# The order of all five engines taken from a list scheduler, in a kernel of decayed attention and a gated layer

## The chip, the cores and the metric

The kernel runs on one core of a Trainium2 chip. Times are microseconds of device time of one execution; the time of a kernel is the median over its runs. The core's engines are TensorE (PE, with its weight loads PEld), VectorE (DVE), ScalarE (ACT), GpSimd (POOL) and SyncE (SP), which here only issues transfers. Each runs its own instructions in the order in which the program wrote them, and waits where an operand is not there yet.

## The reference

Inputs q, k and v have 4 batches, 8 heads, 768 positions and 64 features in float32. With a decay per head, `lam`, and blocks of positions:

```python
intra = einsum(qb, kb) * Dmask;  intra = einsum(intra, vb)
inter = einsum(qb * lam_pow, kv_state)
out[block] = intra + inter
kv_state = lam_block * kv_state + einsum(kb * rev_pow, vb)
```

The attention output, with its 8 x 64 features side by side, is x with 3072 rows of 512, and the gated layer makes the result of it:

```python
H = maximum(x @ w_h, 0);  T = sigmoid(x @ w_t + b_t)
return T * H + (1 - T) * x
```

## The kernel before, in words

Work goes by chunks of 128 positions: 6 in a batch, 24 in all. The heads are taken in 4 pairs, so that a pair's features fill 128 partitions. Decay is factored: values are scaled by a negative power of lam (`pow_k`), the products are taken without decay, and the sum is scaled by a positive power (`pow_q`), so that the mask is a plain triangle (`tri`).

For chunk n the stages are, with the lines of the kernel before:

- SP loads keys (L55), values (L60), and for each pair of chunks the queries (L65). The 8 pieces of the two weight matrices come between chunk 1 and chunk 2 (L85). Up to `LA` = 10 chunks lie ready.
- POOL casts keys (`cast_k`, L140) and queries (`cast_q`, L153) to bf16 and scales values (`scale_v`, L145).
- PE transposes keys (L166) and queries (L159) into one PSUM buffer `tr`; ACT copies them out (`kT` L168, `qT` L161).
- PE makes scores (L179), DVE masks them (L182). PE multiplies the state by the queries (`inter`, L189) and adds the masked scores times the values (`intra`, L196); DVE scales that by `pow_q` into `xT` (L202).
- PE adds the chunk to the state (L211), ACT copies it for the next chunk (`s_bd`, L215).

Two chunks form a group for the gated layer; the last two chunks are groups of one. For a group, in two halves of the output features, PE multiplies by w_h (L223, an h half), DVE takes maximum and difference (`hmx`, L226), PE multiplies by w_t (L235, a t half), ACT takes the sigmoid (L239), DVE multiplies (`thmx`, L242). Then for each chunk PE turns the sum of `xT` and `thmx` back to rows (`ffn_out`, L250, a turn), ACT copies it out (`o_sb`, L254; DVE L256 for two of the last), and SP stores it (L257). Each PSUM tile has one buffer, so an h half waits for the `hmx` of the one before it.

The order on each engine is that of the calls at the end of the function (L279 to L342): a written start for chunks 0 to 4, then a loop whose step i casts chunk i + 3, transposes the keys of i + 2, makes the scores of i + 1, does the rest of i, transposes the next query pair in even steps, does one half of the gated layer (`ffn_step`, L261) with one turn between its h and its t, and loads chunk i + 10. The gated layer takes a group from a list, `units`, that `close` fills (L273). ACT makes the table `pow_q` in eight operations (L126).

Of the kernel before, what the change touches and what calls it, by code (L numbers as in the profile page):

```python
# [12 lines left out]
ALU = mybir.AluOpType  # L13


@with_exitstack
def kernel(
# [20 lines left out]
    LA = 10  # L38
    sizes = [2] * (N // 2 - 1) + [1, 1]
    first = [sum(sizes[:g]) for g in range(len(sizes))]  # L40
    group = [g for g, z in enumerate(sizes) for _ in range(z)]

    ctx.enter_context(tc.manual_schedule())
    singles = ctx.enter_context(tc.tile_pool(name="singles", bufs=1))
    load = ctx.enter_context(tc.tile_pool(name="load", bufs=2))
    work = ctx.enter_context(tc.tile_pool(name="work", bufs=2))
    ps = ctx.enter_context(tc.tile_pool(name="ps", bufs=1, space=bass.MemoryType.PSUM))


    kf, vf, qf = {}, {}, {}  # L50

    def load_k(n):
        b, c = divmod(n, NCH)
        kf[n] = load.tile([C, H, D], F32, tag="kf", name="kf", bufs=LA)
        nc.sync.dma_start(out=kf[n], in_=k[b, :, c * C:(c + 1) * C, :].rearrange("h p d -> p h d"))  # L55

    def load_v(n):
        b, c = divmod(n, NCH)
        vf[n] = load.tile([C, H, D], F32, tag="vf", name="vf", bufs=LA)
        nc.sync.dma_start(out=vf[n], in_=v[b, :, c * C:(c + 1) * C, :].rearrange("h p d -> p h d"))  # L60

    def load_q(s):
        b, c = divmod(J * s, NCH)
        qf[s] = load.tile([128, H, J * D], F32, tag="qf", name="qf", bufs=LA // J)
        nc.sync.dma_start(out=qf[s], in_=q[b, :, c * C:(c + J) * C, :].rearrange("h (p j) d -> p h (j d)", j=J))  # L65

    def loads(n):
        if n < N:
            load_k(n)
            if n % J == 0:  # L70
                load_q(n // J)
            load_v(n)
# [5 lines left out]
    loads(0)  # L78
    loads(1)
    w_f, w_b = [], []  # L80
    for w in (moe_w_h, moe_w_t):
        w_f.append(singles.tile([128, KC, DM], F32, name=f"w_f{len(w_f)}"))
        w_b.append(singles.tile([128, KC, DM], BF16, name=f"w_b{len(w_b)}"))
        for kc in range(KC):
            nc.sync.dma_start(out=w_f[-1][:, kc, :], in_=w[kc * 128:(kc + 1) * 128, :])  # L85
    wh, wt = w_b
    for n in range(2, LA):
        loads(n)


# [10 lines left out]

# [21 lines left out]

    def powers(lo, hi):
        for hp in range(NP):
            nc.scalar.activation(pow_q[:, hp, lo:hi], tq_f[:, lo:hi], AF.Exp, scale=ln_hp[:, hp:hp + 1])  # L126

# [5 lines left out]
    nc.vector.tensor_copy(bt_col, bt_ps)  # L133


    kb, qb, qT, kT, vs, masked, xT, thmx, kv_ps, o_ps = ({} for _ in range(10))

    def cast_k(n, eng=None):
        kb[n] = work.tile([C, H, D], BF16, tag="kb", name="kb", bufs=4)
        (eng or nc.gpsimd).tensor_copy(kb[n], kf[n])  # L140

    def scale_v(n):
        c = n % NCH
        vs[n] = work.tile([C, H, D], BF16, tag="vs", name="vs", bufs=4)
        nc.gpsimd.tensor_tensor(vs[n], in0=vf[n], in1=pow_k[:, :, c, :].to_broadcast([C, H, D]), op=ALU.mult)  # L145

    def cast_q(s, engs=None):
        qb[s] = work.tile([128, J, H, D], BF16, tag="qb", name="qb")
        engs = engs or [nc.gpsimd]
        w = H // len(engs)  # L150
        for i, eng in enumerate(engs):
            h = slice(i * w, i * w + w)
            eng.tensor_copy(qb[s].rearrange("p j h d -> p h j d")[:, h], qf[s].rearrange("p h (j d) -> p h j d", j=J)[:, h])  # L153

    def trans_q(s):
        tr = ps.tile([128, NP, J, 128], BF16, tag="tr", name="tr")
        for hp in range(NP):
            for j in range(J):
                nc.tensor.transpose(tr[:, hp, j, :], qb[s][:, j, 2 * hp:2 * hp + 2, :], id128)  # L159
        qT[s] = work.tile([128, NP, J * C], BF16, tag="qT", name="qT")  # L160
        nc.scalar.activation(qT[s].rearrange("p n (q j) -> p n q j", j=J), tr.rearrange("p n j q -> p n q j"), AF.Copy)  # L161

    def trans_k(n):
        tr = ps.tile([128, NP, C], BF16, tag="tr", name="tr")
        for hp in range(NP):
            nc.tensor.transpose(tr[:, hp, :], kb[n][:, 2 * hp:2 * hp + 2, :], id128)  # L166
        kT[n] = work.tile([128, NP, C], BF16, tag="kT", name="kT", bufs=3)
        nc.scalar.activation(kT[n], tr, AF.Copy)  # L168

    def q_of(n, r, hp):  # L170
        o = n % J * C
        return qT[n // J][r, hp, o:o + C]

    def scores(n):
        s_ps = ps.tile([C, 2, NP, C], F32, tag="s", name="s_ps")
        for hp in range(NP):
            for e in range(2):
                r = slice(64 * e, 64 * e + 64)
                nc.tensor.matmul(s_ps[:, e, hp, :], lhsT=kT[n][r, hp, :], rhs=q_of(n, r, hp), start=True, stop=True)  # L179
        masked[n] = work.tile([C, 2, NP, C], BF16, tag="masked", name="masked")  # L180
        for e in range(2):
            nc.vector.tensor_tensor(masked[n][:, e], in0=s_ps[:, e],  # L182
                                    in1=tri.to_broadcast([C, NP, C]), op=ALU.mult)

    def inter(n):
        o_ps[n] = ps.tile([128, NP, C], F32, tag="o", name="o_ps")
        if n % NCH:
            for hp in range(NP):
                nc.tensor.matmul(o_ps[n][:, hp, :], lhsT=s_bd[n % 2][:, hp, :], rhs=q_of(n, slice(0, 128), hp),  # L189
                                 start=(hp == 0), stop=False, skip_group_check=True)  # L190

    def intra(n):
        c = n % NCH
        for hp in range(NP):
            for e in range(2):
                nc.tensor.matmul(o_ps[n][64 * e:64 * e + 64, hp, :], lhsT=vs[n][:, 2 * hp + e, :], rhs=masked[n][:, e, hp, :],  # L196
                                 start=(hp == 0 and c == 0), stop=True, skip_group_check=True)
        g = group[n]
        r = n - first[g]
        if r == 0:  # L200
            xT[g] = work.tile([128, NP, sizes[g] * C], BF16, tag=f"xT{sizes[g]}", name="xT", bufs=3)
        nc.vector.tensor_tensor(xT[g][:, :, r * C:(r + 1) * C], in0=o_ps[n], in1=pow_q[:, :, c * C:(c + 1) * C], op=ALU.mult)  # L202

    def state(n):
        b, c = divmod(n, NCH)
        if c == NCH - 1:
            return
        if c == 0:
            kv_ps[b] = ps.tile([128, NP, 128], F32, tag="kv", name="kv_ps")
        for hp in range(NP):  # L210
            nc.tensor.matmul(kv_ps[b][:, hp, :], lhsT=kb[n][:, 2 * hp:2 * hp + 2, :], rhs=vs[n][:, 2 * hp:2 * hp + 2, :],  # L211
                             start=(c == 0 and hp == 0), stop=True, skip_group_check=True)
        for e in range(2):
            r = slice(64 * e, 64 * e + 64)
            nc.scalar.activation(s_bd[(n + 1) % 2][r, :, r], kv_ps[b][r, :, r], AF.Copy)  # L215


    def ffn_h(g, js):
        T = sizes[g] * C
        h_ps = ps.tile([128, len(js), T], F32, tag="h", name="h_ps")  # L220
        for i, j in enumerate(js):
            for kc in range(KC):
                nc.tensor.matmul(h_ps[:, i, :], lhsT=wh[:, kc, j * 128:(j + 1) * 128], rhs=xT[g][:, kc, :],  # L223
                                 start=(kc == 0), stop=(kc == KC - 1))
        hmx = work.tile([128, len(js), T], BF16, tag=f"hmx{len(js)}", name="hmx")
        nc.vector.scalar_tensor_tensor(hmx, in0=h_ps, scalar=0.0, in1=xT[g][:, js[0]:js[-1] + 1, :],  # L226
                                       op0=ALU.max, op1=ALU.subtract)
        return hmx

    def ffn_t(g, js, hmx):  # L230
        T = sizes[g] * C
        t_ps = ps.tile([128, len(js), T], F32, tag="t", name="t_ps")
        for i, j in enumerate(js):
            for kc in range(KC):
                nc.tensor.matmul(t_ps[:, i, :], lhsT=wt[:, kc, j * 128:(j + 1) * 128], rhs=xT[g][:, kc, :],  # L235
                                 start=(kc == 0), stop=(kc == KC - 1))
        t_sb = work.tile([128, len(js), T], BF16, tag=f"t_sb{len(js)}", name="t_sb")
        for i, j in enumerate(js):
            nc.scalar.activation(t_sb[:, i, :], t_ps[:, i, :], AF.Sigmoid, bias=bt_col[:, j:j + 1])  # L239
        if js[0] == 0:  # L240
            thmx[g] = work.tile([128, NP, T], BF16, tag=f"thmx{sizes[g]}", name="thmx")
        nc.vector.tensor_tensor(thmx[g][:, js[0]:js[-1] + 1, :], in0=t_sb, in1=hmx, op=ALU.mult)  # L242
# [18 lines left out]
    def ffn_step(eng="act"):  # L261
        unit = units.pop(0) if units else None
        if unit:
            hmx = ffn_h(*unit)
# [53 lines left out]
    for n in range(LA, LA + 2):  # L318
        loads(n)
# [53 lines left out]
```

## Time and profile before

| | us |
|---|---|
| median of 3 runs | 126.14 |
| lowest and highest run | 124.84, 126.16 |
| profiled execution, its time | 125.1 |
| profiled execution, span from first to last instruction | 123.3 |
| PE busy, of the span | 101.0 |
| DVE, ACT, POOL busy | 79.5, 81.9, 56.4 |

In the rows of the profile a line of an engine shows when an instruction started, how long it took, the tiles that it wrote and read, and in brackets how long the engine had been idle before it and what ended that. In the table of stretches each engine has its busy time in that stretch, and the columns behind POOL are the granted TensorE clock (1.00 is full), the share of the DMA engines and what they moved in GB/s. A stretch can hold more than 1.00 of DMA share, since packets overlap.

### The profile page before, as it was taken

The numbers are of one execution on the slowest core, as the hardware profiler recorded it, in microseconds if no ns is written. First come the engines' busy times: TensorE is split into PE (matmuls) and PEld (weight loads), VectorE is DVE, ScalarE is ACT, GpSimd is POOL, SyncE is SP. The second block draws the span as 40 slices with busy tenths as digits, with TensorE's granted clock in tenths as the row PEclk, the third lists the DMA queues.
The fourth block names the chain that finished last, engine by engine and source line by source line (L and its number), as shares of the span: only waits on it lengthen the run. The fifth ranks groups of instructions, "written<-read, shape, count | busy, mean of one in ns | idle before, by whom it ended". The sixth has DMA issues, their size and how long they took to land.

```text
span 123.3 us, 3388 instructions
## 1 busy us (share of the span) xinstructions
PE 101.0 (82%) x1345; PEld 84.1 (68%) x1345; DVE 79.5 (64%) x135; ACT 81.9 (66%) x165; POOL 56.4 (46%) x73
## 2 busy tenths in 40 slices
PE   0236896756819999999999999999999999999930
PEld 0124465535617878898888888888878888888920
DVE  3414851482742698887869978579687997785340
ACT  4647894737623488787885878879588687645550
POOL 6057337728385584819556294193572720000000
PEclk9999999999985999999999999999999999999996
DMA  1999999998999999899999999999999972222233
GB/s 22 276 222 351 363 268 216 250 197 201 258 210 254 217 254 236 226 298 231 263 246 277 243 232 275 235 238 293 244 258 283 311 276 88 85 85 90 85 140 116
DMA packets 67175, 27.48 MB, mean 223 GB/s; under 512 B 50772, under 2 KB 63064, under 8 KB 67160
## 3 DMA queue, kind: packets, MB, share of 16 engines
q1 hardware_dynamic: 67008, 27.27, 92.3%
q8 instruction: 10, 0.16, 0.6%
q14 instruction: 5, 0.04, 0.1%
q10 hardware_dynamic: 152, 0.01, 0.1%
HBM read 20.98 MB, written 6.29 MB: 221 GB/s over the span
## 4 chain that ended last, share of the span: by engine, by line
PE 57%; SPq 18%; DMA 8%; ACT 6%; DVE 4%; issue 2%; POOL 2%; POOLq 0%
PE h_ps L223 14%; PE t_ps L235 14%; SPq L60 9%; PE x_ps L250 7%; SPq L55 6%; DMA vf<-in_v_dram 5%; PE tr L159 5%; PE o_ps L196 4%; ACT t_sb L239 4%; PE s_ps L179 4%; DMA w_f<-in_moe_w_h_dram 4%; PE kv_ps L211 3%; PE o_ps L189 3%; SPq L65 2%; PE tr L166 2%
## 5 line engine op out<-in xcount | busy, mean ns | idle before, releaser
L145 POOL TENSOR_TENSOR vs<-vf,pow_k 128x512 bf16<-128x512 f32 x24 | 25.7, 1071 | 26.4 <-DMA vf<-in_v_dram 20.7
L182 DVE TENSOR_TENSOR masked<-s_ps,tri 128x512 bf16<-128x512 f32 x48 | 30.7, 680 | 6.9 <-PE s_ps L179 6.9
L242 DVE TENSOR_TENSOR thmx<-t_sb,hmx 128x512 bf16<-128x512 bf16 x24 | 15.4, 643 | 21.1 <-ACT t_sb L239 20.9
L239 ACT ACTIVATE t_sb<-t_ps,bt_col 128x256 bf16<-128x256 f32 (+1 forms) x52 | 20.8, 455 | 11.7 <-PE t_ps L235 11.7
L223 PE MATMUL h_ps<-xT,w_b 128*128 128x256 bf16 (+1 forms) x208 | 26.7, 276 | 0.2 <-POOL w_b L300 0.2
L235 PE MATMUL t_ps<-xT,w_b 128*128 128x256 bf16 (+1 forms) x208 | 25.7, 269 | 0.0
L223 PEld LDWEIGHTS <-w_b 128*128 128x128 bf16 x208 | 18.8, 101 | 2.9 <-issue 0.4
L226 DVE SCALAR_TENSOR_TENSOR hmx<-h_ps,xT 128x512 bf16<-128x512 f32 x24 | 16.3, 678 | 6.9 <-PE h_ps L223 6.9
L235 PEld LDWEIGHTS <-w_b 128*128 128x128 bf16 x208 | 18.9, 100 | 2.2
L215 ACT ACTIVATE s_bd<-kv_ps 64x256 bf16<-64x256 f32 x40 | 15.1, 378 | 7.4 <-PE kv_ps L211 6.3
L254 ACT ACTIVATE o_sb<-x_ps 128x512 f32<-128x512 f32 x22 | 13.1, 597 | 8.5 <-PE x_ps L250 8.4
L140 POOL CAST kb<-kf 128x512 bf16<-128x512 f32 x23 | 14.5, 631 | 6.0 <-PE kv_ps L211 3.0
L202 DVE TENSOR_TENSOR xT<-o_ps,pow_q 128x512 bf16<-128x512 f32 x24 | 16.3, 678 | 0.8 <-PE o_ps L196 0.7
L153 POOL CAST qb<-qf 128x1024 bf16<-128x1024 f32 (+1 forms) x12 | 13.1, 1088 | 8.0 <-DMA qf<-in_q_dram 8.0
L161 ACT ACTIVATE qT<-tr 128x1024 bf16<-128x1024 bf16 x12 | 12.3, 1024 | 6.0 <-PE tr L159 5.8
L168 ACT ACTIVATE kT<-tr 128x512 bf16<-128x512 bf16 x24 | 14.3, 597 | 0.7 <-PE tr L166 0.5
L250 PE MATMUL x_ps<-id,xT 128*128 128x128 bf16 x96 | 13.4, 219 | 1.3 <-ACT o_sb L254 0.7
L250 PE MATMUL x_ps<-id,thmx 128*128 128x128 bf16 x96 | 13.4, 219 | 0.2 <-DVE thmx L242 0.2
L159 PE MATMUL tr<-id,qb 128*128 128x128 bf16 x96 | 8.2, 233 | 6.3 <-POOL qb L153 3.4
L159 PEld LDWEIGHTS <-qb 128*128 128x128 bf16 x96 | 6.6, 103 | 7.9 <-POOL qb L153 4.5
L166 PE MATMUL tr<-id,kb 128*128 128x128 bf16 x96 | 9.8, 227 | 2.3 <-DVE kb L140 0.8
L179 PE MATMUL s_ps<-qT,kT 64*128 64x128 bf16 x192 | 10.0, 226 | 2.0 <-ACT qT L161 1.1
(42 smaller groups left out, 96.0 us busy)
## 6 DMA issues: line engine op xcount, KB each, us to landing
kf<-in_k_dram SPq DMA_DIRECT2D x24, 256.0 KB, 5.3
qf<-in_q_dram SPq DMA_DIRECT2D x12, 512.0 KB, 5.7
vf<-in_v_dram SPq DMA_DIRECT2D x24, 256.0 KB, 5.8
out_dram<-o_sb SPq DMA_DIRECT2D x24, 256.0 KB, 3.8
w_f<-in_moe_w_h_dram SPq DMA_DIRECT2D x4, 256.0 KB, 4.4
w_f<-in_moe_w_t_dram SPq DMA_DIRECT2D x4, 256.0 KB, 5.0
lam_bc<-in_lam_dram ACTq DMA_DIRECT2D x1, 4.0 KB, 3.2
bt_r<-in_moe_b_t_dram ACTq DMA_DIRECT2D x1, 2.0 KB
```

The lines of the kernel that those rows point to most:

```text
L145: nc.gpsimd.tensor_tensor(vs[n], in0=vf[n], in1=pow_k[:, :, c, :].to_broadcast([C, H, D]), op=ALU.mult)
L159: nc.tensor.transpose(tr[:, hp, j, :], qb[s][:, j, 2 * hp:2 * hp + 2, :], id128)
L179: nc.tensor.matmul(s_ps[:, e, hp, :], lhsT=kT[n][r, hp, :], rhs=q_of(n, r, hp), start=True, stop=True)
L182: nc.vector.tensor_tensor(masked[n][:, e], in0=s_ps[:, e], in1=tri.to_broadcast([C, NP, C]), op=ALU.mult)
L202: nc.vector.tensor_tensor(xT[g][:, :, r * C:(r + 1) * C], in0=o_ps[n], in1=pow_q[:, :, c * C:(c + 1) * C], op=ALU.mult)
L215: nc.scalar.activation(s_bd[(n + 1) % 2][r, :, r], kv_ps[b][r, :, r], AF.Copy)
L223: nc.tensor.matmul(h_ps[:, i, :], lhsT=wh[:, kc, j * 128:(j + 1) * 128], rhs=xT[g][:, kc, :], start=(kc == 0), stop=(kc == KC - 1))
L226: nc.vector.scalar_tensor_tensor(hmx, in0=h_ps, scalar=0.0, in1=xT[g][:, js[0]:js[-1] + 1, :], op0=ALU.max, op1=ALU.subtract)
L235: nc.tensor.matmul(t_ps[:, i, :], lhsT=wt[:, kc, j * 128:(j + 1) * 128], rhs=xT[g][:, kc, :], start=(kc == 0), stop=(kc == KC - 1))
L239: nc.scalar.activation(t_sb[:, i, :], t_ps[:, i, :], AF.Sigmoid, bias=bt_col[:, j:j + 1])
L242: nc.vector.tensor_tensor(thmx[g][:, js[0]:js[-1] + 1, :], in0=t_sb, in1=hmx, op=ALU.mult)
L250: nc.tensor.matmul(x_ps[:, j * 128:(j + 1) * 128], lhsT=t[:, j, r * C:(r + 1) * C], rhs=id128, start=(j == 0 and i == 0), stop=(i == 1), s ...
```

## The change

The calls at the end are gone. Each stage of each chunk becomes a `Task` with an engine, a duration, a key, and the tiles that it reads and writes, and `plan` seats them one after the other by list scheduling: of all engines it takes the one that can start a task soonest, and on that engine the first by key of those that can start at once. Buffers count: a task that opens a tile waits until the tile that had the buffer is used up. Loads and stores pass through a model of the DMA engines, PE's durations are 1.9 times as long until it has been busy, and a change of array shape on PE costs 0.1. The program is then written in the order of the starts.

```diff
-    i = 2
-    while i < N or units or outs:
...
+    for t in plan(tasks):
+        t.emit()
...
+KQ, KK, KS, KF, KO, KST = 1.2, 0.6, 0.5, 2.5, 4.0, 0.0
+WA = (2, 2)
+OUT_DVE = (21, 23)
...
+            w_done[w].append(task(eng, 0.6, w_after[w] - 1 + 0.01 * (w * KC + kc),
...
+            task("PE", 0.445, n - KQ, lambda s=s: trans_q(s), reads=[("qb", s)], writes=[("qtr", s), ("qT", s)])
+            for eng, x in [("ACT", slice(0, 64)), ("DVE", slice(64, 128))] if s == 0 else [("ACT", slice(0, 128))]:
...
+        task("PE", 0.23, n - KS, lambda n=n: scores(n), mode=1, reads=[("kT", n), ("qT", s)], writes=[("s", n), ("m", n)])
+        task("DVE", 1.28, n - 0.5, lambda n=n: mask(n), reads=[("s", n)], writes=[("m", n)])
...
+                f = n + KF + u * 0.5
...
+                parts = 2 if m == N - 1 else 1
...
+                    eng = ("ACT", "DVE")[i] if parts > 1 else "DVE" if m in OUT_DVE else "ACT"
...
+                    task("SP", 0.5, m + KST, lambda m=m, i=i, js=js: store(m, i, js), reads=[("o_sb", m, i)], size=0.7 / parts)
```

What else differs: `qT` has three buffers instead of two; the copy of the first query pair out of PSUM is split between ACT and DVE; the gated layer of the two groups of one chunk runs in halves like the others; the last chunk is turned, copied (one half on ACT, one on DVE) and stored in two halves, the second in the PSUM buffer of `t`; and the masks, copies and casts are tasks of their own, so that an engine may take another task between a product and what follows it. The instructions on PE are the same number, 1345 products.

Three places show the new order. On DVE, at the start: first what came after the cast of the first queries (`qb`) before, then what comes now. `masked` and `m` are the masked scores, `xT` the scaled sums, `w_b0` and `w_b1` the cast weights.

```order
L153 CAST qb_175<-qf_75 128x4x2x64
L182 TENSOR_TENSOR masked_205<-s_ps_196,tri_140 128x512 x2
L202 TENSOR_TENSOR xT_232<-o_ps_223,pow_q_166 128x4x128
L182 TENSOR_TENSOR masked_252<-s_ps_243,tri_140 128x512 x2
L294 CAST w_b0_84<-w_f0_83 128x512 x2
```

```order
L298 CAST qb_134<-qf_114 128x4x2x64
L311 COPY qT_163<-tr_143 128x4x128
L273 CAST w_b0_110<-w_f0_108 128x512
L337 TENSOR_TENSOR m_197<-s_172,tri_75 128x512 x2
L273 CAST w_b0_110<-w_f0_108 128x512
L353 TENSOR_TENSOR xT2_231<-o_210,pow_q_101 128x4x128
```

The first weight cast stands ahead of the first mask now, the second ahead of the first scaled sum.

On PE, around the first half of group 1 of the gated layer (chunks 2 and 3). Of each block of like products the first is shown. `kv` is the state, `tr` a transpose, `h` and `t` the two halves, `x` a turn; before, from chunk 4's state update on:

```order
L211 MATMUL kv_ps_234<-vs_387,kb_383 128x128
...
L159 MATMUL tr_577<-id128_135,qb_476 128x128
...
L223 MATMUL h_ps_588<-xT_435,w_b0_84 128x256
...
L235 MATMUL t_ps_599<-xT_435,w_b1_90 128x256
...
L166 MATMUL tr_625<-id128_135,kb_533 128x128
```

and now, from chunk 4's state update on:

```order
L358 MATMUL kv_157<-vs_419,kb_350 128x128
...
L303 MATMUL tr_432<-id128_70,qb_382 128x128
...
L347 MATMUL o_414<-m_411,vs_327 64x128
...
L388 MATMUL x_453<-id128_70,xT2_231 128x128
...
L369 MATMUL h_467<-xT2_391,w_b0_110 128x256
...
L332 MATMUL s_482<-qT_464,kT_421 128x128
```

Before, query pair 3 (`qb_476`, chunks 6 and 7) was transposed ahead of that h half; now only pair 2 (`qb_382`) is, and chunk 4's state update stands ahead of pair 2, of chunk 3's intra product (`o_414`) and of the first turn.

On SP, around the first stores: before, all loads up to chunk 11 stood ahead of the first store; now two stores stand among chunk 8's loads. Before, chunks 10 and 11 and the first store:

```order
L55 DMA kf_389<-in_k_dram 128x8x64
L65 DMA qf_391<-in_q_dram 128x8x128
L60 DMA vf_393<-in_v_dram 128x8x64
L55 DMA kf_395<-in_k_dram 128x8x64
L60 DMA vf_397<-in_v_dram 128x8x64
L257 DMA out_0_dram<-o_sb_463 128x512
```

and now, chunk 8 and the first two stores:

```order
L316 DMA kf_480<-in_k_dram 128x8x64
L399 DMA out_0_dram<-o_sb1_476 128x512
L293 DMA qf_531<-in_q_dram 128x8x128
L399 DMA out_0_dram<-o_sb1_529 128x512
L316 DMA vf_593<-in_v_dram 128x8x64
```

Ahead of the last load stood ten stores; now sixteen do.

More of the change, by code (lines that the diff above doesn't have):

```diff
@@ L147, in cast_q @@
[L147 to L153, printed above, removed]
+    w_f = [singles.tile([128, KC, DM], F32, name=f"w_f{i}") for i in range(2)]
+    w_b = [singles.tile([128, KC, DM], BF16, name=f"w_b{i}") for i in range(2)]
@@ new lines, with half, load_w, cast_w @@
+    V, A, P, T = nc.vector, nc.scalar, nc.gpsimd, nc.tensor
+    def half(e):
+        return slice(64 * e, 64 * e + 64)
+    def load_w(w, kc):
+        nc.sync.dma_start(out=w_f[w][:, kc, :], in_=(moe_w_h, moe_w_t)[w][kc * 128:(kc + 1) * 128, :])
+    def cast_w(eng, w, kc):
+        if eng == "ACT":
+            A.activation(w_b[w][:, kc, :], w_f[w][:, kc, :], AF.Copy)
+        else:
+            {"DVE": V, "POOL": P}[eng].tensor_copy(w_b[w][:, kc, :], w_f[w][:, kc, :])
+    w_done = [[], []]
@@ L181, in scores, with mask @@
+    def mask(n):
         for e in range(2):
[L182 to L183 removed]
+            V.tensor_tensor(get("m", n)[:, e], in0=get("s", n)[:, e], in1=tri.to_broadcast([C, NP, C]), op=ALU.mult)
     def inter(n):
[L186 to L190, printed above, removed]
+        for hp in range(NP):
+            T.matmul(get("o", n)[:, hp, :], lhsT=s_bd[n % 2][:, hp, :], rhs=q_of(n, slice(0, 128), hp),
+                     start=(hp == 0), stop=False, skip_group_check=True)
@@ new lines, in decay, with state @@
+    def decay(n):
+        g, c = group[n], n % NCH
+        r = n - first[g]
+        V.tensor_tensor(get("xT", g)[:, :, r * C:(r + 1) * C], in0=get("o", n), in1=pow_q[:, :, c * C:(c + 1) * C], op=ALU.mult)
+    def state(n):
+        b, c = divmod(n, NCH)
+        for hp in range(NP):
+            T.matmul(get("kv", b)[:, hp, :], lhsT=get("kb", n)[:, 2 * hp:2 * hp + 2, :], rhs=get("vs", n)[:, 2 * hp:2 * hp + 2, :],
+                     start=(c == 0 and hp == 0), stop=True, skip_group_check=True)
@@ L230, in ffn_t @@
[L230 to L242, printed above, removed]
```

459 lines of the change are left out of this document (285 added, 174 removed).

## The prediction

> **What bounds the kernel now.** I read the page's busy shares and slices first, then the stretches, then the chain of waits, then the timeline of the stretches that stand out. TensorE (PE) is the busiest engine and its slices are full from the thirteenth on, while the DMA slices are full until about 98 us:
>
> ```profile
> PE 101.0 (82%) x1345; PEld 84.1 (68%) x1345; DVE 79.5 (64%) x135; ACT 81.9 (66%) x165; POOL 56.4 (46%) x73
> PE   0236896756819999999999999999999999999930
> DMA  1999999998999999899999999999999972222233
> ```
>
> The span is 123.3 us, so PE is idle for 22.3 us. The stretches say where:
>
> ```profile
> core 0: us, PE busy (x) PEld busy (x) DVE busy (x) ACT busy (x) POOL busy (x), PEclk, DMA share, GB/s
> 20.00:25.00 5.00, 3.44 (x44) 2.88 (x44) 2.05 (x4) 3.10 (x6) 3.68 (x5) 1.00 1.23 240
> 25.00:30.00 5.00, 2.58 (x45) 1.96 (x43) 2.88 (x5) 2.72 (x5) 2.71 (x3) 1.00 0.97 201
> 30.00:35.00 5.00, 3.61 (x63) 2.58 (x60) 3.44 (x6) 3.34 (x8) 2.17 (x3) 1.00 1.13 235
> 35.00:40.00 5.00, 3.42 (x23) 2.74 (x24) 0.97 (x2) 1.02 (x1) 3.69 (x5) 0.66 1.09 233
> 40.00:45.00 5.00, 4.81 (x73) 3.89 (x71) 3.64 (x7) 2.71 (x7) 3.47 (x4) 1.00 1.22 223
> ...
> 110.00:115.00 5.00, 4.78 (x71) 4.44 (x70) 2.65 (x5) 2.38 (x6) 0.00 (x0) 1.00 0.28 104
> 115.00:120.00 5.00, 3.31 (x53) 2.89 (x50) 2.40 (x5) 2.74 (x9) 0.00 (x0) 1.00 0.32 119
> ```
>
> From 20 to 40 us PE is idle for 7.0 us, and from 35 to 40 it also runs at a granted clock of 0.66. After 45 it is full to 110. The end of the steady part therefore moves only if PE comes to 45 us with more work behind it. To count work I price each block by one row of the chain of waits, from a stretch in which PE has no gap (start, duration, what):
>
> ```profile
> 48.98 0.87 PE h_ps L223 x8
> 49.85 0.45 PE x_ps L250 x8
> 50.30 0.87 PE t_ps L235 x8
> 51.17 0.22 PE tr L166 x4
> 51.39 0.22 PE o_ps L189 x4
> 51.62 0.33 PE s_ps L179 x8
> 51.95 0.34 PE o_ps L196 x8
> 52.29 0.33 PE kv_ps L211 x4
> 52.62 0.57 PE tr L159 x8
> ```
>
> In order: one h half, one output turn, one t half, the transposes of a key chunk, state times queries, scores, the intra product, the state update, the transposes of a query pair. The whole program by these prices: 24 x (0.22 + 0.33 + 0.34 + 0.45) + 20 x (0.22 + 0.33) + 12 x 0.57 + 44 x 0.87 + 3.6 for the two groups of one chunk = 91.9 us. PE's floor is that; everything above it is waiting or a slow clock.
>
> **Why it is idle there.** Not for want of data, but of order:
>
> ```profile
> 28.82 0.22 PE L250 MATMUL x_ps<-id,thmx 128*128 128x128 bf16 x1
> ...
> 31.95 0.68 DVE L202 TENSOR_TENSOR xT<-o_ps,pow_q 128x512 bf16<-128x512 f32 x1
> ...
> 33.67 0.40 PE L211 MATMUL kv_ps<-vs,kb 128*128 128x128 bf16 x4
> ...
> 35.48 1.04 POOL L153 CAST qb<-qf 128x1024 bf16<-128x1024 f32 x1
> ...
> 36.58 1.03 PE L159 MATMUL tr<-id,qb 128*128 128x128 bf16 x8 [2.51 <-POOL qb L153]
> 37.41 1.91 PE L223 MATMUL h_ps<-xT,w_b 128*128 128x256 bf16 x8
> ...
> 44.73 0.61 PE L159 MATMUL tr<-id,qb 128*128 128x128 bf16 x8 [0.19 <-ACT kT L168]
> ```
>
> At 33.67 PE has nothing left in its queue that it may run: next stands the transpose of query pair 3, whose cast ends at 36.52, and behind it in the same queue stand the h and t halves of group 1, whose input (chunks 2 and 3) had been there since 32.63, the end of the DVE row. The gap of 2.51 us also costs clock: this h half took 1.91 us, not 0.87. When query pair 4 is transposed at 44.73, PE has done, by the order's count, 9 key transposes, 4 query transposes, 8 scores, 5 state products, 7 intra products, 6 state updates, 8 halves of h and t, and 2 turns: 20.2 us of work in 44.7 us.
>
> **The change, part by part.** Same instructions, bytes and buffers nearly; their order is new.
>
> *Start.* On VectorE (DVE) the cast of the second weight piece now stands ahead of the first mask. Before, that mask ran as soon as scores existed:
>
> ```profile
> 10.30 1.29 DVE L182 TENSOR_TENSOR masked<-s_ps,tri 128x512 bf16<-128x512 f32 x2 [2.89 <-PE s_ps L179]
> ...
> 12.73 0.61 POOL L294 CAST w_b<-w_f 128x512 bf16<-128x512 f32 x1 [0.61 <-DMA w_f<-in_moe_w_h_dram]
> ...
> 16.06 1.86 PE L223 MATMUL h_ps<-xT,w_b 128*128 128x256 bf16 x8 [0.24 <-POOL w_b L300]
> ...
> 17.33 0.61 POOL L140 CAST kb<-kf 128x512 bf16<-128x512 f32 x1 [1.30 <-DMA kf<-in_k_dram]
> ```
>
> The third weight piece landed at 12.7 (row at 12.73, which waited 0.61 us for it), and the first had landed before the cast ahead of that row, by 11.5; so the second lands near 12.0 (an estimate), its cast takes some 0.4 (less than POOL's 0.61, an estimate too), and the mask starts near 12.4 instead of 10.3, and the first intra product, PE's next, waits with it. ScalarE (ACT) has six of its eight power tables ahead of the first query copy; the copy, split in two with DVE, may come late by them, but under a microsecond of that hides beneath the mask's 2.1. PE's key transpose of chunk 2 now stands ahead of the first h half, and its cast ends at 17.94, so the h half starts near 18.4 instead of 16.06: 2.4 us later. Behind it come, until the wait for chunk 4's values, 6.6 us of blocks at full clock, some 9.1 with a first h half at 1.86, the same doubling for what follows it in the first 3.4 us, and a table load on ACT. That is 27.5. What comes next on PE is chunk 4's state update, which needs the scaled values that end at 29.0 in the old trace (same loads in the same order, same POOL order up to there):
>
> ```profile
> 20.40 1.24 POOL L145 TENSOR_TENSOR vs<-vf,pow_k 128x512 bf16<-128x512 f32 x1 [0.18 <-DMA vf<-in_v_dram]
> ...
> 26.88 1.04 POOL L153 CAST qb<-qf 128x1024 bf16<-128x1024 f32 x1 [2.36 <-DMA qf<-in_q_dram]
> 27.95 1.06 POOL L145 TENSOR_TENSOR vs<-vf,pow_k 128x512 bf16<-128x512 f32 x1
> ...
> 41.53 1.06 POOL L145 TENSOR_TENSOR vs<-vf,pow_k 128x512 bf16<-128x512 f32 x1 [2.54 <-PE o_ps L196]
> ...
> 48.01 1.06 POOL L145 TENSOR_TENSOR vs<-vf,pow_k 128x512 bf16<-128x512 f32 x1 [2.11 <-DMA vf<-in_v_dram]
> ...
> 95.05 1.06 POOL L145 TENSOR_TENSOR vs<-vf,pow_k 128x512 bf16<-128x512 f32 x1 [2.17 <-DMA vf<-in_v_dram]
> ```
>
> So the delay of the start costs nothing as long as the 1.5 us between 27.5 and 29.0 cover it; without that cover each microsecond comes out at the end. At 29.0 both orders stand alike: 10.5 us of work done before (end of the first turn, row at 28.82), 10.0 after.
>
> *The middle.* From there the new PE order has, up to chunk 8's state update: 3 state updates, 3 query and 4 key transposes, 5 intra products, 5 scores, 3 state products, 7 halves and 4 turns = 15.5 us, and no block that comes before its data by the arrivals of the old trace, but for some 0.3 us at chunks 6 and 7. It reaches chunk 8 at 29.0 + 15.8 = 44.8, with 25.5 us of work done, not 20.2. That is the gain: 5.3 us.
>
> *Clock.* The gap before 29.0 is some 1.5 to 2 us. A gap of 2.51 us halved the clock (above); the gaps in 25 to 30, 2.42 us in several pieces, did not. I take no loss, and keep 1.5 us (1.91 - 0.87 and 1.03 - 0.57) for the range: the span below would be 120.5. The Trainium skill ("TensorE: Matmul & The Clock Gate", What's actually happening) puts the half clock after about one whole idle window of 3.4 us; by that neither gap would be punished, and the trace already shows one of 2.51 us that was, so the measurement decides; by the page the span would stay as summed.
>
> *Steady part.* Scores and intra products use half of the array's rows or columns. A state update behind an intra product takes 0.33 us where four like matmuls among their own kind take 0.22, so a change of shape costs 0.11. The old order changes 75 times, the new 84: + 1.0 us. The old order needed 74.9 us (44.73 to 119.62) for its last 71.7 us of work, 3.2 over; I keep that. 44.8 + (91.9 - 25.5) + 1.0 + 3.2 = 115.4.
>
> *Loads.* SP's queue has two stores ahead of chunk 8's last load and about one with every later chunk; before, ten stores stood ahead of the last load, now sixteen.
>
> ```profile
> 46.50 1.03 SPq L257 DMA_DIRECT2D out_dram<-o_sb  x1
> ```
>
> Values of chunks 2 to 10 were scaled 27.6 us apart, 3.45 a chunk, without stores; those of 10 to 22 47.0 us apart with nine stores between, so a store costs (47.0 - 12 x 3.45) / 9 = 0.62. Chunk 8's values, scaled from 41.53 before, come at 41.5 + 2 x 0.62 + 1.06 = 43.8 at the latest, a microsecond ahead of PE. Chunk 19, the tightest, has ten stores behind that: 43.8 + 11 x 3.45 + 10 x 0.62 = 88.0. PE needs it after 40.8 us of blocks and their part of the 4.2 over: 88.2. So data and PE run side by side, and I put 0.7 us for loads that come late here and there; 0 at the low end. If a store costs what its row shows in the queue, 1.03, chunk 19 comes at 92.8, 4.6 us late.
>
> *Tail.* The last groups run in halves, and the last chunk is turned, copied and stored in halves. Waits in 110 to 120 were 1.9 us; 0.4 of that is after the last matmul, and of the 1.5 left I keep 1.0: - 0.5. Last rows of the chain:
>
> ```profile
> 119.00 0.62 PE x_ps L250 x8
> ...
> 119.64 0.69 DVE o_sb L256
> ```
>
> From 119.62 to 123.3 is 3.7 us; half a copy is 0.40 (between 0.35, half of 0.69, and 0.69), and a store of half the size is left at 2.97: 3.4.
>
> Sum: 115.4 - 0.5 + 3.4 + 0.7 = **119.0 us of span, 4.3 less**. The profiled execution took 125.1, 1.8 beyond its span, and the median of the runs is 126.14, 1.04 above that execution: 119.0 + 1.8 + 1.04 = **121.8 us**.
>
> **Rivals.** *The loads set the pace.* Without the 0.7 but with 4.6 us of late data at chunk 19 the span is 122.9, the time 125.7. For it: DMA slices are full to 98 us, and POOL still waits over 2 us for values at 48.01 and at 95.05. Against: with nine stores in twelve chunks the pace was 3.92, all in. *Margins (slower).* The new order leaves 2.0 to 2.2 us of PE work between a chunk's scores and its intra product, the old one 3.5 to 4.0. The mask takes 1.29, and DVE may have two other operations of 0.68 (as the row at 31.95) ahead of it: 2.8 with hand-overs, so 0.5 us of wait in each of 16 chunks would be 8.0 us: span 127.0, time 129.8. It decides from 0.35 us a chunk (4.3 us gained and 1.3 of bound, over 16). Against it: DVE is busy for 64% of the span only, so a mask rarely finds two operations ahead of it. *The start is not covered.* If cold clock and ACT's queue push chunk 4 to 32 instead of 29, 3.0 us come out at the end: 124.8. That the order is not changed at all is excluded by its rows.
>
> **How the numbers follow.** Forecast 0.78, loads 0.10, margins 0.07, start 0.05. One per cent, 1.26 us, is about what this measurement tells from no change; its bounds are 124.9 and 127.4. Faster: the forecast and 0.04 of start and loads that end below 124.9, 0.82; same 0.11; slower 0.07. Low end: no load waits, no price for shapes, 1.3 us less at the tail and start: 116.0 of span, 118.8. High end: the loads' rival, 125.7.
>
> **What would show it.** Right: first masks near 12.4, first h half near 18.4, PE slices full from about 29 us on, h half of group 2 before 40 us, group 1's before 32; stores from about 35 us; the last value load landing after 101; a last half copy of about 0.4. Wrong: waits of PE for masks in most chunks after 45 (margins), POOL or PE waiting for values beyond 2 us in sum after 60 (loads), a granted clock below 0.9 in a slice after 25 (clock), or chunk 8's state update after 47 (start).

## The result, and the profile after

| | before | after |
|---|---|---|
| median of the runs measured side by side, us | 126.15 (4 runs, 124.84 to 126.71) | 121.92 (4 runs, 121.21 to 122.65) |
| profiled execution, us | 125.1 | 121.64 |
| its span, us | 123.3 | 119.9 |

The ratio is 0.968, with a 95% interval of 0.958 to 0.978: faster, by 4.2 us. The forecast was 121.8.

The page of the kernel after, with the busy time of TensorE and its 40 slices:

```profile
PE 101.3 (84%) x1345; PEld 82.4 (69%) x1345; DVE 78.5 (65%) x140; ACT 79.9 (67%) x166; POOL 56.4 (47%) x73
PE   0247549997999999999399999999799999999970
PEclk9999999999999999999999999999999999999999
DMA  0999999999998998999979999989999989902442
```

PE's busy time is what it was (101.0 before); of 22.3 us of idle time 18.6 are left. PE is now full from the seventh slice (18 us) on but for the tenth, not from the thirteenth. Two slices fall out after that, at 57 to 60 and at 84 to 87 us. The stretches, in the columns of before:

```profile
20.00:25.00 5.00, 5.00 (x39) 3.60 (x36) 0.85 (x2) 3.45 (x6) 3.70 (x5) 1.00 1.23 241
25.00:30.00 5.00, 4.28 (x69) 3.32 (x64) 4.79 (x8) 3.57 (x9) 2.72 (x3) 1.00 0.97 199
30.00:35.00 5.00, 4.77 (x76) 3.85 (x71) 2.72 (x5) 3.62 (x7) 3.31 (x4) 1.00 1.20 245
35.00:40.00 5.00, 5.00 (x72) 4.24 (x67) 4.40 (x8) 3.93 (x10) 2.63 (x4) 1.00 1.00 257
40.00:45.00 5.00, 4.99 (x80) 3.98 (x78) 4.29 (x9) 3.24 (x6) 2.67 (x3) 1.00 1.13 230
50.00:60.00 10.00, 8.14 (x117) 6.82 (x116) 6.98 (x12) 5.92 (x13) 5.38 (x7) 1.00 1.05 267
80.00:90.00 10.00, 9.17 (x123) 7.66 (x121) 7.78 (x14) 6.86 (x16) 5.61 (x7) 1.00 1.02 261
```

PE was idle for 7.0 us between 20 and 40 us before; now it is idle for 0.95. The clock is 1.00 in all of these stretches. New are the 1.86 us missing between 50 and 60, and 0.83 between 80 and 90. The timeline of the kernel after names both, and shows the other places that the prediction spoke of:

```profile
12.28 1.27 DVE L337 TENSOR_TENSOR m<-s,tri 128x512 bf16<-128x512 f32 x2
...
18.55 1.92 PE L369 MATMUL h<-xT,w_b 128*128 128x256 bf16 x8
...
29.05 0.38 PE L358 MATMUL kv<-vs,kb 128*128 128x128 bf16 x4 [0.68 <-POOL vs L319]
...
45.06 0.39 PE L358 MATMUL kv<-vs,kb 128*128 128x128 bf16 x4
...
58.99 0.62 PE L303 MATMUL tr<-id,qb 128*128 128x128 bf16 x8 [1.86 <-POOL qb L298]
...
86.34 0.38 PE L358 MATMUL kv<-vs,kb 128*128 128x128 bf16 x4 [0.78 <-POOL vs L319]
...
116.11 0.22 PE L388 MATMUL t<-id,xT 128*128 128x128 bf16 x1 [0.49 <-ACT t_sb L378]
...
116.56 0.22 PE L388 MATMUL t<-id,th 128*128 128x128 bf16 x1
116.82 0.42 DVE L396 COPY o_sb<-t 128x256 f32<-128x256 f32 x1 [0.44 <-PE t L388]
```

They are, in order: the first mask, the first h half, the state updates of chunks 4 and 8, the transposes of query pair 6, the state update of chunk 18, whose values came late, the last turn, and the last half copy. After 45 us the view of waits shows PE waiting twice for data that was loaded late, 2.64 us in sum, and never for masks. What GpSimd (POOL) had just done before 45.06 shows how closely chunk 8 is met:

```profile
40.73 1.04 POOL L298 CAST qb<-qf 128x1024 bf16<-128x1024 f32 x1 [1.82 <-DMA qf<-in_q_dram]
43.37 1.30 POOL L319 TENSOR_TENSOR vs<-vf,pow_k 128x512 bf16<-128x512 f32 x1 [1.60 <-DMA vf<-in_v_dram]
```

Chunk 8's scaled values end at 44.67 and PE takes them up at 45.06, without a wait. The last loaded operand that PE did wait for before it is chunk 4's values, 0.68 us at 29.05; from there to chunk 8 are 16.0 us, with no wait longer than 0.23.

### The profile page after: what moved, and what is told of

Same layout as the page of the kernel before. It is cut to its first block, busy times and chain, and to the rows that moved or that the text cites. A ratio compares the mean times of both kernels' runs of the same rounds, so it can differ in the third digit from the quotient of the medians.

```text
span 119.9 us, 3415 instructions
## 1 busy us (share of the span) xinstructions
PE 101.3 (84%) x1345; PEld 82.4 (69%) x1345; DVE 78.5 (65%) x140; ACT 79.9 (67%) x166; POOL 56.4 (47%) x73
## 4 chain that ended last, share of the span: by engine, by line
PE 44%; DMA 27%; SPq 13%; POOL 6%; ACT 3%; issue 2%; DVE 1%; ACTq 0%; POOLq 0%
PE h L369 11%; SPq L316 11%; DMA qf<-in_q_dram 10%; PE t L369 10%; DMA vf<-in_v_dram 9%; PE x L388 6%; POOL vs L319 4%; DMA kf<-in_k_dram 4%; PE s L332 4%; PE o L347 3%; DMA w_f<-in_moe_w_h_dram 3%; PE tr L303 3%; PE tr L323 3%; PE o L341 2%; PE kv L358 2%
## 5 line engine op out<-in xcount | busy, mean ns | idle before, releaser
L337 DVE TENSOR_TENSOR m<-s,tri 128x512 bf16<-128x512 f32 x48 | 30.8, 682 | 7.6 <-PE s L332 7.5
L369 PE MATMUL h<-xT,w_b 128*128 128x256 bf16 (+1 forms) x208 | 26.5, 273 | 0.2 <-DVE xT L353 0.2
L369 PE MATMUL t<-xT,w_b 128*128 128x256 bf16 (+1 forms) x208 | 26.1, 270 | 0.0
L373 DVE SCALAR_TENSOR_TENSOR hmx<-h,xT 128x512 bf16<-128x512 f32 (+1 forms) x26 | 16.8, 647 | 13.6 <-PE h L369 13.5
L378 ACT ACTIVATE t_sb<-t,bt_col 128x256 bf16<-128x256 f32 (+1 forms) x52 | 20.9, 454 | 6.9 <-PE t L369 6.4
L353 DVE TENSOR_TENSOR xT<-o,pow_q 128x512 bf16<-128x512 f32 x24 | 16.5, 687 | 5.4 <-PE o L347 5.2
L394 ACT ACTIVATE o_sb<-x 128x512 f32<-128x512 f32 (+1 forms) x23 | 13.5, 587 | 8.4 <-PE x L388 7.4
L363 ACT ACTIVATE s_bd<-kv 64x256 bf16<-64x256 f32 x40 | 15.0, 375 | 3.9 <-PE kv L358 3.3
L388 PE MATMUL x<-id,xT 128*128 128x128 bf16 x94 | 13.2, 220 | 0.0
L388 PE MATMUL x<-id,th 128*128 128x128 bf16 x94 | 13.1, 219 | 0.0
```

The lines of the kernel that those rows point to most:

```text
L337: V.tensor_tensor(get("m", n)[:, e], in0=get("s", n)[:, e], in1=tri.to_broadcast([C, NP, C]), op=ALU.mult)
L353: V.tensor_tensor(get("xT", g)[:, :, r * C:(r + 1) * C], in0=get("o", n), in1=pow_q[:, :, c * C:(c + 1) * C], op=ALU.mult)
L363: A.activation(s_bd[(n + 1) % 2][half(e), :, half(e)], get("kv", n // NCH)[half(e), :, half(e)], AF.Copy)
L369: T.matmul(get(x, g, js[0])[:, i, :], lhsT=w[:, kc, j * 128:(j + 1) * 128], rhs=get("xT", g)[:, kc, :], start=(kc == 0), stop=(kc == KC - 1))
L373: V.scalar_tensor_tensor(get("hmx", g, js[0]), in0=get("h", g, js[0]), scalar=0.0, in1=get("xT", g)[:, js[0]:js[-1] + 1, :], op0=ALU.max, ...
L378: A.activation(get("t_sb", g, js[0])[:, i, :], get("t", g, js[0])[:, i, :], AF.Sigmoid, bias=bt_col[:, j:j + 1])
```

## The experiments

**The theory:** the time is set by how much work PE has done when data arrive that nothing can replace: chunk 8's values, near 45 us. The new order has 25.5 us done there instead of 20.2. The rivals: filling the single worst gap does it; or one other engine's order does it; or it comes from finer interleaving everywhere, whatever is done by 45 us. A second question was what the 2.64 us of waits after 45 are. Each kernel was measured beside the kernel before, whose median was 125.3 to 125.6 in those runs. The kernel after was measured only in the runs of the result, beside 126.15; where a kernel is set against it, the ratios to the kernel before and the rows of the traces carry the argument, since its own interval (0.958 to 0.978) is wide.

### One gap filled in the old order

`swap4` is the kernel before with group 1's h half, turn and t half ahead of query pair 3's transposes, in that one step.

```diff
+        if i == 4:
+            ffn_step()
         if i % J == 0 and i + 2 < N:
             trans_q(i // J + 1)
-        ffn_step("dve" if i >= N and i % 2 else "act")
+        if i != 4:
+            ffn_step("dve" if i >= N and i % 2 else "act")
```

> The old kernel with one place altered: in loop step 4 the half of the gated layer (h and t half of group 1) is written ahead of the transposes of query pair 3. Theory (the gain of the change lies in filling PE's wait of 2.51 us before that transpose, and in keeping the clock): the h half starts near 34 instead of 37.4 and takes 0.9, not 1.91; PE comes to the transpose of query pair 4 between 1.6 and 3.0 us sooner than 44.73, the earlier bound because query pair 4 is cast only by about 43; time 126.1 less 1.6 to 3.0, 123.1 to 124.5. Rival (the gain lies in the tail, the stores or the buffers): no change, 126.1 within 0.6.

Measured: 125.38 us, ratio 0.998 (0.994 to 1.002). No change. Its timeline:

```profile
37.64 0.62 PE L159 MATMUL tr<-id,qb 128*128 128x128 bf16 x8
39.61 0.38 PE L166 MATMUL tr<-id,kb 128*128 128x128 bf16 x4 [1.35 <-ACT qT L161]
45.56 0.62 PE L159 MATMUL tr<-id,qb 128*128 128x128 bf16 x8 [1.59 <-POOL qb L153]
```

Pair 3's transposes wait for nothing now. But the key transpose right behind them waits 1.35 us for the copy that empties `tr`, and pair 4 waits 1.59 us for its cast. Pair 4 starts at 45.56 (44.73 before) with the same 20.2 us done, since the exchange moved nothing across it. The idle time was filled and came back ahead of the next late operand. My expectation had counted the gap and not the work ahead of that operand; the first rival falls with it.

### The same work moved behind chunk 8, in the new order

`late2` is the kernel after, planned with one condition more: group 2's halves of the gated layer may start only after chunk 8's state update. `late12` holds groups 1 and 2 in this way.

```diff
+    for g in (2,):
+        for t in gated[g]:
+            t.after.append(kv_done[8])
     for t in plan(tasks):
```

> The changed kernel, planned with one more condition: the four halves of group 2 of the gated layer may only come after chunk 8's state update. Theory (what counts is the work done when chunk 8's values arrive): 3.5 us of work less are done at 45 us, these come out at the end, less what they cover of the 2.6 us of later waits for loads: 122.8 to 125.4 us. Rival (the gain comes from the finer interleaving of all engines, whatever is done by chunk 8): 121.2 to 122.6.

> The same with groups 1 and 2 held until chunk 8's state update: eight halves and two turns, 7.9 us of work, are not done at 45 us. Theory: 7.9 less at most 2.6 covered, and some half clock in the gaps: 127 to 131 us, slower than the kernel before. Rival (finer interleaving): 121.5 to 124.

Measured: `late2` 123.81 us, ratio 0.985 (0.980 to 0.990); `late12` 127.67 us, ratio 1.019 (1.015 to 1.022), slower than before. The work that moved was less than the expectations said: one t half of group 2 stood behind chunk 8 in the kernel after already, so that by the prices of the prediction 22.9 us are done ahead of chunk 8 in `late2` and 18.2 in `late12`. First `late2`, then `late12`, each with chunk 8's state update and the last matmul:

```profile
44.92 0.40 PE L358 MATMUL kv<-vs,kb 128*128 128x128 bf16 x4
...
118.68 0.22 PE L388 MATMUL t<-id,th 128*128 128x128 bf16 x1
```

```profile
44.36 0.58 PE L358 MATMUL kv<-vs,kb 128*128 128x128 bf16 x4 [0.20 <-POOL vs L319]
...
122.39 0.22 PE L388 MATMUL t<-id,th 128*128 128x128 bf16 x1
```

Chunk 8 comes within 0.7 us of the same time in both and in the kernel after (45.06). What differs is the way from there to the end of the last matmul: 71.7 us after, 74.0 in `late2`, 78.3 in `late12`, for 66.4, 69.0 and 73.7 us of work left of the 91.9. The end follows the work that is left, to within the 5.3, 5.0 and 4.6 us that lie over it. In `late12` PE also pays the clock:

```profile
35.00:40.00 5.00, 3.21 (x58) 2.34 (x56) 4.04 (x7) 3.13 (x6) 3.00 (x4) 1.00 1.05 258
40.00:45.00 5.00, 2.70 (x27) 2.04 (x25) 1.50 (x3) 1.41 (x2) 2.66 (x3) 0.59 1.24 234
45.00:50.00 5.00, 5.00 (x39) 3.67 (x38) 2.20 (x4) 1.69 (x5) 2.70 (x4) 0.73 1.15 241
```

It is idle for 4.1 us from 35 to 45, and at 0.73 of the clock from 45 to 50 it loses 5 x 0.27 = 1.35 us more. In the profiled execution of `late2` a slow clock stands ahead of chunk 8 too (stretches in the last section). It does not explain the time: two other executions of `late2`, at a granted clock of 1.00, took 123.94 and 123.77 us. All other parts of the change are in these kernels, the finer interleaving too; without all of the work ahead of chunk 8, `late2` keeps only part of the gain and `late12` none of it. That rival falls.

Two limits of the theory show in the rows. Of the kernels in the new order only `late12` waits for chunk 8's values themselves, 0.20 us, after waiting 1.69 us for query pair 4; elsewhere chunk 8 is a mark at which the work is counted, in a stretch where the data come one behind the other. And its values can come earlier when SP's order changes: in `hold4b`, below, they are ready at 42.95, and its state update still comes only at 45.52, 15.9 us after chunk 4's.

### The order on GpSimd alone

`q_first` is the kernel before with query pairs cast ahead of the scaled values, as the new order has it. `q_last` is the kernel after, planned with the reverse for pairs 3 to 11.

```diff
-            scale_v(i + 3)
             if i % J and (i + 3) % J == 0:
                 cast_q((i + 3) // J)
+            scale_v(i + 3)
```

```diff
...
+        if n >= 6 and n % J == 0:
+            q_cast.after.append(tasks[-1])
```

> The kernel before with one exchange on GpSimd: in the loop the cast of a query pair stands ahead of the scaled values of the chunk that is loaded behind it, as in the changed kernel's order; nothing else differs. Theory: query pair 3 was cast at 35.48 us behind values that landed at 34.48; its data were there near 33.1 (where the changed kernel casts it), so the transpose comes near 34.2 instead of 36.58, the slow clock behind that gap (1.5 us) goes, and the next pair, cast near 41.8 instead of 43.6, lets 2 to 3 us of it through: 1.8 to 3.2 us faster than the kernel before. Rival (the gap only moves to the next wait, as with the exchange on TensorE): within 0.7 us of the kernel before.

> The changed kernel, planned with one more condition on GpSimd: from pair 3 on, a query pair is cast behind the scaled values of its first chunk, as in the kernel before. Theory: the plan moves other blocks of TensorE ahead of the later queries, so that the order of casts costs little where the blocks follow: 0 to 1.2 us slower than the changed kernel, 121.5 to 123. Rival (the order of casts on GpSimd alone makes the gain): 2.5 to 4 us slower, 124 to 125.7.

Measured: `q_first` 124.89 us, ratio 0.998 (0.993 to 1.002), no change; `q_last` 124.14, ratio 0.985 (0.976 to 0.993), 2.2 us slower than the kernel after by the medians, with intervals that just meet. Both came out where the rival had them, and not for the rival's reason. In `q_first` TensorE:

```profile
35.56 0.61 PE L159 MATMUL tr<-id,qb 128*128 128x128 bf16 x8
...
41.80 0.40 PE L211 MATMUL kv_ps<-vs,kb 128*128 128x128 bf16 x4
...
90.91 0.61 PE L159 MATMUL tr<-id,qb 128*128 128x128 bf16 x8 [1.00 <-ACT kT L168]
```

The gap at pair 3 is gone and chunk 6's state update comes at 41.80; before it came at 44.14. But the last matmul ends only 0.5 us earlier than before (119.11, 119.61). New waits eat the lead; the view of waits from 45 us on has them in one row (total, times, longest), where the kernel before has 0.3:

```profile
PE tr L159 <- ACT kT L168: 2.4, 5, 1.0
```

The transposes of later pairs wait for a copy on ScalarE (ACT). What that copy stood behind, on ACT of the same kernel:

```profile
89.05 0.60 ACT L254 ACTIVATE o_sb<-x_ps 128x512 f32<-128x512 f32 x1 [2.42 <-DMA out_dram<-o_sb]
89.54 0.83 ACT L239 ACTIVATE t_sb<-t_ps,bt_col 128x256 bf16<-128x256 f32 x2
90.25 0.61 ACT L168 ACTIVATE kT<-tr 128x512 bf16<-128x512 bf16 x1
```

The output copy waits 2.42 us for a store to leave one of the six `o_sb` buffers; the key copy, and behind it the query transposes, wait with it. Three such waits make 5.0 us on ACT; the kernel before has none. They stand ahead of three of the five waits of the query transposes, 1.7 of the 2.4 us. So an earlier PE runs into the queue of loads and stores.

In `q_last` the plan moved other blocks up, as I had expected, but not enough: pair 4's transposes, chunk 7's state product and intra product and chunk 8's scores, 1.46 us, fall behind chunk 8's state update, which comes at 45.59. From there to the end of the last matmul it takes 73.6 us, 1.9 more than after:

```profile
45.59 0.39 PE L358 MATMUL kv<-vs,kb 128*128 128x128 bf16 x4
...
118.97 0.22 PE L388 MATMUL t<-id,th 128*128 128x128 bf16 x1
```

So the early cast is a condition for the work ahead of chunk 8, not a gain by itself.

### Loads and stores

In the kernel after SP holds back up to four stores behind later loads (`hold4`; `hold4b` is the same kernel again); those left follow the last load. `half_after` and `half_before` store only half of the rows of the first 20 chunks, and `q_first_half` does that in `q_first`.

```diff
...
     for t in plan(tasks):
+        if t.eng == "SP" and t.reads:
+            held.append(t)
+            if len(held) > 4 or not loads_left:
+                held.pop(0).emit()
+            continue
         t.emit()
...
```

```diff
-        nc.sync.dma_start(out=out[n * C:(n + 1) * C, :], in_=o_sb)
+        r = 64 if n < 20 else C
+        nc.sync.dma_start(out=out[n * C:n * C + r, :], in_=o_sb[0:r])
```

> The scheduled kernel with only SP's queue altered: up to four finished output tiles are held back, so that each store stands about four loads-with-store places later and the last load has 12 stores ahead of it, not 16. Theory (stores ahead of loads make the waits of 1.86 and 0.78 us that PE has for queries and values after 45 us): both waits vanish, the last value load is scaled about 2 us sooner, the span falls from 119.9 to about 117.7, the time from 121.9 to about 119.7. Rival (the waits come from the pace of the loads themselves, 3.45 us a chunk, and not from the stores' place): waits and time stay within 0.5 us of the scheduled kernel. Second rival (the held stores pile up at the end): the last store comes late and the time is at or above 121.9.

> The changed kernel with up to four stores held back behind later loads on SP, the same as hold4, for a profile without a disturbance and a second measurement beside other kernels. By the theory that the loads, delayed by the stores in their queue, are what TensorE waits for after 45 us: 119 to 120.5 us again, and of the 2.6 us of waits after 45 us at most 1 us left, with query pair 6 and the values at 86 us in time. Rival: the order of the queue has no part, the gain of hold4 came from its own runs: 121 to 122.5.

> The changed kernel, in which the stores of the first 20 chunks write only rows 0 to 63 of their chunk (half of these rows of the output is left out); order, loads and computation are the same. By the theory that the stores delay the loads: a store costs the queue half, 16 of them about 5 us less by the last load, and the 2.6 us of waits after 45 us fall below 0.7: 119.0 to 120.5 us. Rival: the waits come from the order of casts on GpSimd and of blocks on TensorE: 121 to 122.5.

> The kernel before, in which the stores of the first 20 chunks write only rows 0 to 63 of their chunk (half of these rows of the output is left out). Theory: TensorE has no wait for loads after 45 us in the kernel before, so faster loads are worth nothing there: within 0.7 us of the kernel before, where the same made the changed kernel 2.2 us faster. Rival (less traffic helps either kernel): 2 us faster.

> The kernel before with query pairs cast ahead of the scaled values (as in q_first) and stores of rows 0 to 63 alone for the first 20 chunks (as in half_before; half of these rows of the output is left out). In q_first chunk 6's state update came 2.3 us earlier than before, and the last matmul only 0.5 earlier. Theory: the lead ran into loads that had not come (key and query data of the later chunks), so with faster loads it comes through: 122.5 to 124.2 us. Rival: the lead is eaten by the old order itself (transposes that wait in one buffer for copies on ScalarE), which faster loads don't change: 124.5 to 125.6.

| | us | ratio to before |
|---|---|---|
| `hold4` | 119.80 | 0.956 (0.947 to 0.965) |
| `hold4b` | 119.44 | 0.955 (0.951 to 0.959) |
| `half_after` | 119.74 | 0.956 (0.953 to 0.960) |
| `half_before` | 125.33 | 0.996 (0.991 to 1.000) |
| `q_first_half` | 122.69 | 0.981 (0.976 to 0.986) |

Where PE waited from 45 us on, in `hold4b` and then in `half_after` (total, times, longest):

```profile
PE t L388 <- ACT t_sb L378: 0.5, 1, 0.5
PE s L332 <- ACT qT L309: 0.5, 1, 0.5
```

```profile
PE tr L303 <- POOL qb L298: 1.3, 1, 1.3
PE t L388 <- ACT t_sb L378: 0.5, 1, 0.5
```

With the stores held back both waits for loads are gone, and the span is 117.5, 2.4 us less than after for 2.64 us of waits. With half the bytes and the old places the wait for pair 6 stays in part, 1.3 where I expected less than 0.7 for all: its load is issued no earlier (51.22; after 50.72; `hold4b` 48.46) and its cast starts no earlier (58.18; 57.89; 53.98). The wait is shorter than after only because PE comes to it 0.8 us later; the wait at chunk 18 is gone. So the place of a store in the queue counts beside its bytes.

By the ratios the same relief is worth 0.6 us in the kernel before, with an interval that reaches zero; the earlier casts alone bring 0.3, within theirs; both together bring 2.4. In `q_first_half` the lead comes through, with chunk 6's state update 3.1 us earlier than before and the last matmul 2.7:

```profile
41.01 0.40 PE L211 MATMUL kv_ps<-vs,kb 128*128 128x128 bf16 x4
...
116.67 0.22 PE L250 MATMUL x_ps<-id,thmx 128*128 128x128 bf16 x1
```

Two limits lie one behind the other: the old order hid the queue, and taking one away shows the other. I had expected the lead of `q_first` to meet late keys and queries; its rows show late output buffers first, and the runs don't separate the two. ACT's waits for stores are still 2.9 us in `q_first_half`, where PE's waits for the key copy behind 45 are 0.8 us.

### Start and tail undone

`start_old` is the kernel after with the first masks and sums ahead of the weight casts on DVE and the first h half ahead of chunk 2's key transpose. `tail_whole` is it with the last chunk and the groups of one chunk in one piece.

```diff
+        if t.eng == "DVE" and made[("m", 0)] in t.writes:
+            late[0].emit()
...
+        if t.eng == "PE" and made[("h", 0, 0)] in t.writes:
+            trk2.emit()
```

```diff
-            w = 1 if z == 4 else 2
+            w = 4 if z == 1 else 2
...
-                parts = 2 if m == N - 1 else 1
+                parts = 1
```

> The scheduled kernel with its start put back: on DVE the two first masks and the first two scaled sums stand ahead of the weight casts that were put before them, and on PE the first h half stands ahead of chunk 2's key transpose. Theory (the late start is covered, since PE then waits for chunk 4's scaled values, which end at 29.0 us whatever PE does): the first h half starts near 16.3 instead of 18.55, chunk 4's state update stays at 29.0 to 29.1, PE's wait before it grows from 0.68 to about 2.5 us, and the time stays within 0.4 us of 121.9. Rival (the start's delay comes out at the end): 1.5 to 2.2 us faster, about 120. If the longer wait halves the clock: up to 1.5 us slower.

> The scheduled kernel with its tail undone: the two groups of one chunk run as one block of 16 products each for h and t, and the last chunk is turned, copied and stored whole. Theory (the tail brought 0.5 us of waits and 0.3 us at the last copy and store): 0.8 us slower than the scheduled kernel, 122.7. Rival (the tail carries a large part of the gain of 4 us): 2 us slower or more, 124 and above.

Measured: `start_old` 122.11 us (0.974, 0.966 to 0.982), the kernel after's time within its interval; `tail_whole` 123.33 (0.985, 0.976 to 0.994). First `start_old`, then `tail_whole`:

```profile
17.01 1.86 PE L369 MATMUL h<-xT,w_b 128*128 128x256 bf16 x8 [0.78 <-DVE xT L353]
...
21.07 1.03 PE L303 MATMUL tr<-id,qb 128*128 128x128 bf16 x8 [1.67 <-POOL qb L298]
```

```profile
117.67 0.22 PE L388 MATMUL x<-id,xT 128*128 128x128 bf16 x1 [0.69 <-ACT o_sb L394]
...
118.06 0.22 PE L388 MATMUL x<-id,th 128*128 128x128 bf16 x1
118.32 0.69 DVE L396 COPY o_sb<-x 128x512 f32<-128x512 f32 x1 [1.52 <-PE x L388]
```

The h half comes 1.5 us earlier, and PE waits 1.67 us for query pair 1 behind it: the late start costs nothing, as forecast, only the cover stands at another place than chunk 4's values, where I had expected it. In `tail_whole` 3.7 us follow the last matmul (span 122.0, last end 118.28) instead of 3.1, and from chunk 8 (45.96) to there it takes 72.3, not 71.7. But 0.4 of that difference is longer waits for loads (3.07, not 2.64): from chunk 20's state update on, behind the last of these waits, it takes 23.0 us (from 95.25), not 22.6 (from 94.16). So the halves are worth about 0.4 + 0.6 = 1.0 us. By the medians it is 1.4; the 0.9 us by which that execution reached chunk 8 later than the kernel after's are not of the tail.

## Why the prediction was right

- **Start: right.** First mask 12.28 (12.4 forecast), first h half 18.55 (18.4), chunk 4's state update 29.05 (29.0). PE came there at 28.4, not 27.5, so the cover was 0.68 us and not 1.5; it was enough.
- **Middle: right, and shown.** Chunk 8 at 45.06 (44.8) with 25.5 us done. `late2`, `q_last` and `late12` took 2.6, 1.5 and 7.3 us of work away from ahead of it, and the way from there to the last matmul grew by 2.3, 1.9 and 6.6, with chunk 8 at 44.4 to 45.6 in all of them. Its values were nearer than forecast: ready at 44.67, not at 43.8 "at the latest", so 0.4 us ahead of PE and not a microsecond.
- **Clock: right for this kernel, but no law.** No stretch from 20 to 117 us is below 1.00. The last section shows that gaps of the same length cost clock in other kernels.
- **Steady part: the two terms over the work were too large.** From chunk 8 to the end 66.4 us of work were left, and I put 1.0 for shapes and 3.2 kept from before on top. Of the 71.7 us measured, 66.4 are work, 2.64 waits for loads, 0.49 the wait in the tail; 2.2 remain. With the tail's wait that is 2.7, where I had 4.2 less 0.5. The 3.2 kept from before held 1.3 us of waits at the old end, two of its turns that waited 0.60 and 0.69 for output copies, of which I had taken off only 0.5.
- **Loads: too small.** 2.64 us instead of 0.7. The mechanism was that of the first rival, though not at chunk 19: pair 6's queries at 58.99 were late first, 1.86 us, and I had followed only the values of chunks 8 and 19. `hold4b` shows the price, 2.4 us of span. My sign for this rival, POOL or PE waiting for values beyond 2 us in sum after 60, was badly chosen: POOL waits 8.0 us for them there, but 10.6 in the kernel before, while PE's own wait is 0.78.
- **Tail and end.** About 1.0 us for the halves by `tail_whole`; I had 0.5 and 0.3. After the last matmul 3.1, not 3.4.
- **From span to median.** The span came out at 119.9, 0.9 above the forecast; the median lies 0.3 above the profiled execution, not 1.04. These two cancel, as the loads (1.9 too little) and the terms over the work (1.0 too much) do in part, so the 121.8 is nearer than its parts: the mechanism stands, the closeness is in part luck.

## What to carry to other kernels

Look for the stretch in which operands come so late that the order on the engine cannot bring them forward, and count the work that the engine has done by then. Here only work moved ahead of it counted, and filling a gap before it with work that was ahead of it already brought nothing. Before a part is undone or done alone, look for a second limit right behind the first: earlier casts and lighter stores brought 0.3 and 0.6 us alone, and 2.4 together. In a full queue look at a store's place as well as its bytes: up to four stores held back behind later loads took the kernel after from 121.9 to 119.4 us (ratios 0.968 and 0.955), as much as halving the bytes of its first 20 stores did (119.7), and faster than both kernels.

## What the hardware showed unexpectedly

Gaps of the same length don't always cost the same clock. Both `hold4b` and `late2` waited 2.08 us ahead of chunk 4's state update. Stretches of `hold4b`, then of `late2`:

```profile
28.00:30.00 2.00, 0.42 (x8) 0.42 (x8) 0.61 (x2) 0.14 (x1) 1.92 (x3) 1.00 0.97 212
30.00:32.00 2.00, 1.77 (x29) 1.40 (x27) 0.69 (x1) 1.89 (x4) 1.63 (x3) 1.00 1.05 269
```

```profile
28.00:30.00 2.00, 0.66 (x7) 0.65 (x7) 0.38 (x2) 0.00 (x0) 1.84 (x2) 0.73 0.89 200
30.00:32.00 2.00, 2.00 (x23) 1.63 (x21) 0.61 (x1) 1.78 (x3) 1.63 (x2) 0.50 1.01 254
```

The clock stayed at 1.00 in the one and fell to 0.50 in the other; in `q_last` it fell to 0.50 in the same stretch after a gap of 1.50 us. The Trainium skill ("TensorE: Matmul & The Clock Gate", What's actually happening) has the half clock after one idle window of about 3.4 us that runs free of the program. That it runs free would fit two outcomes for one gap; that it must be idle for 3.4 us does not fit gaps of 1.50 and 2.08, and here the measurement decides.
